# Decode attention on one core: value loads on a second queue, loads emitted four steps ahead, and the softmax maximum on TensorE

## The chip, the cores and the metric

The kernel runs on one core of a Trainium2 chip. The metric is device time in microseconds (us), as the median of several executions. The span on a profile page is one execution as the hardware profiler saw it; it is about 2 us shorter than the timed number. Most executions of a kernel agree within a per cent. An execution that is over 1.5% above the fastest of the same kernel is called slow and is left out of ratios.

## The reference, cut to what matters

One token attends over the last 4096 positions of a cache with 32 heads of size 128. A small MLP runs beside it, and its output gates the result.

```python
def _A_ref(x, k_cache, v_cache, wq, wo):          # x: 1 x 1 x 512
    W = min(4096, max(256, Sk // 4))              # Sk = 32768, W = 4096
    q = (x @ wq) ...                              # 32 heads x 128
    k = k_cache[:, :, Sk - W:, :]                 # 32 x 4096 x 128, bf16
    v = v_cache[:, :, Sk - W:, :]
    scores = einsum("bhqd,bhkd->bhqk", q, k) * Dh ** -0.5
    p = softmax(scores)
    return einsum("bhqk,bhkd->bhqd", p, v) ... @ wo
# ... the MLP is cut
return attention(layernorm(x)) * silu(mlp(x))
```

Keys and values are 32 x 2 tiles of 1 MiB. Each is read once and used for a few microseconds.

## The kernel before

Heads are taken in eight groups of four (`G = 4`). The scores of an even head are computed on VectorE. Those of an odd head take 32 transposes on TensorE, copies on ScalarE and 32 matrix-vector products. After the fourth key of a group comes the softmax. Values follow four heads later (`LAG = 4`). I write K28 for the key tile of head 28 and V28 for its value tile; "the Exp of group 6" is the softmax exponential of heads 24 to 27.

```python
def load(dst, src):
    return tc.keep_in_program_order(nc.sync.dma_start(out=dst, in_=src))   # all on SP's queue
...
def k_head(h, kn):
    if h % 2 == 0:                                   # VectorE: multiply, then sum over d
        nc.vector.tensor_tensor(out=prod[:], in0=kn[:], in1=q_bc[...], op=ALU.mult)
        nc.vector.tensor_reduce(out=s["sS"][...], in_=prod[:], axis=AX.X, op=ALU.add)
    else:                                            # TensorE transposes, ScalarE copies
        for b in range(NB):
            for i in range(8):
                nc.tensor.transpose(pt[:, i, :], kn[:, b * 8 + i, :], ident_bf[:])
            nc.scalar.copy(out=kt[:, b * 8:(b + 1) * 8, :], in_=pt[:])
        ...                                          # then qk(): 32 small matmuls
    if hl == G - 1:
        softmax(g)

def softmax(g):
    ...                                              # m1: maxima of each partition
    nc.gpsimd.partition_all_reduce(mb[:], m1[:], channels=P, reduce_op=ReduceOp.max)
    ...                                              # subtract, then on ScalarE:
    nc.scalar.activation(out=pT[:], in_=e[:], func=ACT.Exp, scale=scale)
...
for i in range(H + LAG):
    if i < H:
        k_head(i, load_kv(k_pool, A_k_cache, i))     # 12 key buffers
    ...
    if i >= LAG:
        h = i - LAG
        v = load_kv(v_pool, A_v_cache, h)            # 7 value buffers
        ...
        v_head(h, v)                                 # 32 matmuls of one head
```

So all loads stand in one queue, in the order in which they are needed: K4, V0, K5, V1 and so on.

## Time and profile before

| | before |
|---|---|
| time, median of 3 first runs | 198.48 us (198.36 to 199.85) |
| span of the profiled execution | 196.8 us |
| bytes moved | 79.17 MB |
| busy: TensorE, VectorE, ScalarE, GpSimd | 61%, 64%, 35%, 3% |
| mean granted TensorE clock | 0.667 of full speed |

The page of the kernel before shows how the loads are spread. A queue line gives packets, megabytes and the share of the 16 DMA engines' time. An issue line gives the count, the size of one and the median time from issue to landing:

```profile
q1 hardware_dynamic: 11176, 78.85, 96.3%
...
kv<-in_A_k_cache_dram SPq DMA_DIRECT2D x32, 1024.0 KB, 19.7
kv<-in_A_v_cache_dram SPq DMA_DIRECT2D x32, 1024.0 KB, 19.7
```

The reader should see one queue at 96% of the DMA engines' time, and a load that lands 19.7 us after its issue. At 424 GB/s a tile takes 2.47 us, so some eight loads are always in flight. The prediction shows three more views of this kernel: the strip (the span in 40 equal slices, with the busy share of the DMA engines in tenths and what they moved in GB/s), the ending chain (the work that ended last, followed back from step to step to what released it, as shares of the span), and the tail, which is the end of the timeline. The issue lines tell that keys and values are treated alike.

### The profile page before, as it was taken

Reading aid. Unit: us, or ns where it says so; the run is one execution under the profiler, and the core shown is the slowest. Engines: PE = TensorE matmul, PEld = TensorE weight load, DVE = VectorE, ACT = ScalarE, POOL = GpSimd, SP = SyncE. Lnnn points to the kernel's source line nnn. Section 1 sums busy time; section 2 is a strip of 40 time slices with the busy share of each in tenths; the row PEclk is TensorE's granted clock in tenths of the full one; section 3 lists DMA queues with packets and bytes.
Section 4 is the critical chain, followed back from the end, with each engine's and each line's share of the span. In section 5 each row is a group of like instructions: output and inputs, shape, how many; then the busy total and the mean of one; then the engine's idle time right before and its main releaser. Section 6 shows DMA issues by size and latency. Waiting matters only on the chain.

```text
span 196.8 us, 5237 instructions
## 1 busy us (share of the span) xinstructions
PE 119.4 (61%) x2399; PEld 108.4 (55%) x2399; DVE 126.9 (64%) x140; ACT 69.3 (35%) x82; POOL 4.9 (3%) x17
## 2 busy tenths in 40 slices
PE   0315896851969474684829293756665654929443
PEld 0314745841969473583829292656565653929332
DVE  1225049998959993959387937959198929594301
ACT  2000329742565243070707070242525250707000
POOL 1011000000000000000000000000000000000000
PEclk9999999695585555576766667555555585575555
DMA  6999899999999999999999999999999999999960
GB/s 185 383 485 446 355 416 421 426 426 421 426 421 423 421 421 425 423 425 420 426 421 428 421 425 416 425 420 426 423 428 423 425 418 425 421 426 422 426 268 10
DMA packets 11349, 79.17 MB, mean 402 GB/s; under 512 B 1376, under 2 KB 1984, under 8 KB 2368
## 3 DMA queue, kind: packets, MB, share of 16 engines
q1 hardware_dynamic: 11176, 78.85, 96.3%
q8 instruction: 18, 0.29, 0.6%
q10 hardware_dynamic: 152, 0.00, 0.0%
q14 instruction: 3, 0.02, 0.0%
HBM read 78.84 MB, written 0.00 MB: 401 GB/s over the span
## 4 chain that ended last, share of the span: by engine, by line
DMA 71%; DVE 12%; issue 6%; PE 6%; ACT 2%; POOL 1%; SPq 0%; POOLq 0%
DMA kv<-in_A_v_cache_dram 40%; DMA kv<-in_A_k_cache_dram 30%; DVE sS L265 7%; DVE prod L262 3%; ACT kt L272 1%; PE a_ps L202 1%; PE qT_ps L221 1%; PE oT L364 1%; PE qb_ps L230 1%; PE h_ps L135 1%; PE y_ps L135 0%; PE ln_ps L140 0%; PE ln_ps L152 0%; ACT q_bc L232 0%; POOL ln_rstd_x L158 0%
## 5 line engine op out<-in xcount | busy, mean ns | idle before, releaser
L272 ACT COPY kt<-pt 128x1024 bf16<-128x1024 bf16 x64 | 60.2, 1025 | 73.0 <-PE pt L271 73.0
L265 DVE TENSOR_REDUCE sS<-prod 128x32 f32<-128x4096 bf16 x16 | 70.7, 4419 | 0.5
L271 PE MATMUL pt<-ident_bf,kv 128*128 128x128 bf16 x512 | 53.8, 298 | 18.2 <-DMA kv<-in_A_k_cache_dram 17.7
L271 PEld LDWEIGHTS <-kv 128*128 128x128 bf16 x512 | 49.8, 140 | 19.7 <-DMA kv<-in_A_k_cache_dram 18.7
L364 PEld LDWEIGHTS <-kv 128*128 128x128 bf16 x1024 | 30.0, 102 | 30.5 <-DMA kv<-in_A_v_cache_dram 22.8
L262 DVE TENSOR_TENSOR prod<-kv,q_bc 128x4096 bf16<-128x4096 bf16 x16 | 36.5, 2283 | 11.0 <-DMA kv<-in_A_k_cache_dram 8.8
L364 PE MATMUL oT<-pT,kv 128*128 128x1 bf16 x1024 | 32.6, 165 | 17.6 <-DMA kv<-in_A_v_cache_dram 17.3
L243 PE MATMUL sT<-qT_bf,kt 128*128 128x1 bf16 x512 | 20.4, 166 | 2.6 <-ACT kt L272 2.3
L243 PEld LDWEIGHTS <-kt 128*128 128x128 bf16 x512 | 18.3, 103 | 3.4 <-ACT kt L272 3.2
L300 PE MATMUL den_ps<-pT,ones_bf 128*128 128x128 bf16 x8 | 2.0, 253 | 16.9 <-ACT pT L294 16.9
L371 DVE TENSOR_TENSOR o<-oT,rden 128x4 bf16<-128x4 f32 x7 | 1.1, 162 | 17.3 <-PE oT L364 17.3
L294 ACT ACTIVATE pT<-e 128x128 bf16<-128x128 f32 x8 | 2.5, 309 | 16.5 <-DVE e L290 16.5
L140 PEld LDWEIGHTS ln_ps<-x_f,ones_f 128*128 128x128 f32 x4 | 1.0, 312 | 11.3 <-DVE x_f L182 6.4
L287 POOL PARTITION_ALL_REDUCE mb<-m x8 | 3.0, 373 | 162.5 <-DVE m L285 162.5
L205 ACT ACTIVATE a_bf<-a_ps 128x10 bf16<-128x10 f32 x1 | 0.2, 180 | 17.4 <-PE a_ps L202 17.4
L302 DVE TENSOR_REDUCE den<-den_ps 128x4 f32<-128x128 f32 x8 | 2.3, 292 | 5.5 <-PE den_ps L300 5.5
L135 PEld LDWEIGHTS <-ox 128*1 128x1 bf16 x112 | 2.5, 113 | 5.3 <-DVE ox L341 5.3
L367 DVE TENSOR_TENSOR o<-oT,rden 128x1 bf16<-128x1 f32 x4 | 0.6, 161 | 7.2 <-PE oT L364 7.2
L230 PE MATMUL qb_ps<-wq_sb,xn_rep 128*128 128x512 bf16 x16 | 5.2, 497 | 0.0
L135 PE MATMUL y_ps<-wo,ox 128*1 128x128 bf16 x112 | 3.7, 306 | 2.3 <-DVE ox L341 2.3
L140 PE MATMUL ln_ps<-x_f,ones_f 128*128 128x4 f32 x4 | 1.2, 365 | 5.9 <-DVE x_f L163 4.9
L290 DVE TENSOR_TENSOR e<-sS,mb 128x64 f32<-128x64 f32 x8 | 1.8, 224 | 3.9 <-POOL mb L287 3.9
(79 smaller groups left out, 48.2 us busy)
## 6 DMA issues: line engine op xcount, KB each, us to landing
kv<-in_A_k_cache_dram SPq DMA_DIRECT2D x32, 1024.0 KB, 19.7
kv<-in_A_v_cache_dram SPq DMA_DIRECT2D x32, 1024.0 KB, 19.7
wq_sb<-in_A_wq_dram SPq DMA_DIRECT2D x1, 4096.0 KB, 19.2
wo<-in_A_wo_dram SPq DMA_DIRECT2D x3, 1024.0 KB, 20.4
w_sb<-in_B_w_dram SPq DMA_DIRECT2D x1, 1376.0 KB, 7.9
w_sb<-in_B_w_dram SPq DMA_DIRECT2D x1, 1024.0 KB, 10.2
w_sb<-in_B_w_dram SPq DMA_DIRECT2D x1, 512.0 KB, 3.7
wo<-in_A_wo_dram SPq DMA_DIRECT2D x1, 512.0 KB, 19.8
```

The costliest lines, as they stand in the source:

```text
L135: nc.tensor.matmul(ps[32 * j:32 * j + 1, :], lhsT=col, rhs=w[0:k, j * P:(j + 1) * P], start=False, stop=last, skip_group_check=True)
L140: nc.tensor.matmul(ps[:], lhsT=ones_f[:], rhs=src_f, start=True, stop=True)
L230: nc.tensor.matmul(qb_ps[:], lhsT=xn_rep[:, c, :], rhs=wq_h[:, c, 2 * i:2 * i + 8:2, :], start=(c == 0), stop=(c == KC - 1))
L243: nc.tensor.matmul(sT[:, hl // 2, c:c + 1], lhsT=kt[:, c, :], rhs=qT_bf[:, h:h + 1], start=True, stop=True)
L262: nc.vector.tensor_tensor(out=prod[:], in0=kn[:], in1=q_bc[:, h // 2:h // 2 + 1, :].to_broadcast([P, NC, Dh]), op=ALU.mult)
L265: nc.vector.tensor_reduce(out=s["sS"][:, hl // 2, :], in_=prod[:], axis=AX.X, op=ALU.add)
L271: nc.tensor.transpose(pt[:, i, :], kn[:, b * 8 + i, :], ident_bf[:])
L272: nc.scalar.copy(out=kt[:, b * 8:(b + 1) * 8, :], in_=pt[:])
L287: nc.gpsimd.partition_all_reduce(mb[:], m1[:], channels=P, reduce_op=ReduceOp.max)
L294: nc.scalar.activation(out=pT[:], in_=e[:], func=ACT.Exp, scale=scale)
L302: nc.vector.tensor_reduce(out=den[:], in_=den_ps[:], axis=AX.X, op=ALU.add)
L364: nc.tensor.matmul(oT[:, k:k + 1], lhsT=v[:, c, :], rhs=s["pT"][:, hl % 2, hl // 2, c:c + 1], start=(c == 0), stop=(c == NC - 1))
```

## The change

It has three parts. Keys stay on SP's queue and values go to ScalarE's (ACT), which should let two issuers work side by side. Loads are emitted four loop steps ahead of their use. The maximum over partitions goes from GpSimd's all-reduce to a transpose and a matmul on TensorE.

```diff
-    def load(dst, src):
-        return tc.keep_in_program_order(nc.sync.dma_start(out=dst, in_=src))
+    def load(dst, src, q=None):
+        return tc.keep_in_program_order((q or nc.sync).dma_start(out=dst, in_=src))
 ...
+    ident_f = const.tile([P, P], FP32, name="ident_f")
+    make_identity(nc, ident_f[:])
 ...
-        nc.gpsimd.partition_all_reduce(mb[:], m1[:], channels=P, reduce_op=ReduceOp.max)
+        mt_ps = ps_misc.tile([G, P], FP32, tag="misc", name="mt_ps")
+        nc.tensor.transpose(mt_ps[:], m1[:].rearrange("p a b -> p (a b)"), ident_f[:])
+        mx = sm_pool.tile([G, 1], FP32, tag="mx", name="mx")
+        nc.vector.tensor_reduce(out=mx[:], in_=mt_ps[:], axis=AX.X, op=ALU.max)
+        md = sm_pool.tile([G, G], FP32, tag="md", name="md")
+        nc.vector.tensor_scalar(out=md[:], in0=ident_f[0:G, 0:G], scalar1=mx[:], ...)
+        mb_ps = ps_misc.tile([P, G], FP32, tag="misc", name="mb_ps")
+        nc.tensor.matmul(mb_ps[:], lhsT=ones_f[0:G, :], rhs=md[:], start=True, stop=True)
+        nc.vector.tensor_copy(out=mb[:], in_=mb_ps[:].rearrange("p (a b) -> p a b", a=2))
 ...
+    def loads(i):
+        if i < H:
+            kt_in[i] = load_kv(k_pool, A_k_cache, i, nc.sync)
+        if LAG <= i < H + LAG:
+            h = i - LAG
+            vt_in[h] = load_kv(v_pool, A_v_cache, h, nc.scalar)
 ...
+    for i in range(PF):                              # PF = 4
+        loads(i)
 ...
     for i in range(H + LAG):
+        loads(i + PF)
 ...                                                  # k_head and v_head as before
```

More of the change, by code (lines that the diff above doesn't have):

```diff
@@ L7 @@
 from concourse.masks import make_identity
-from concourse.bass_isa import ReduceOp
 P = 128
@@ L21 @@
 LAG = 4
+PF = 4
 K_BUFS = 12
@@ L90, with load_kv @@
     load(wq_sb[:], A_wq.rearrange("(p c) n -> p c n", p=P))
-    def load_kv(pool, cache, h):
+    def load_kv(pool, cache, h, q):
         t = pool.tile([P, NC, Dh], BF16, tag="kv", name="kv")
-        load(t[:], cache[0, h, W0:, :].rearrange("(p c) d -> p c d", p=P))
+        load(t[:], cache[0, h, W0:, :].rearrange("(p c) d -> p c d", p=P), q)
         return t
@@ L286, in softmax @@
         mb = sm_pool.tile([P, 2, G // 2], FP32, tag="mb", name="mb")
-        nc.gpsimd.partition_all_reduce(mb[:], m1[:], channels=P, reduce_op=ReduceOp.max)
+        mt_ps = ps_misc.tile([G, P], FP32, tag="misc", name="mt_ps")
[3 more added lines that the diff above has]
+        md = sm_pool.tile([G, G], FP32, tag="md", name="md")
+        nc.vector.tensor_scalar(out=md[:], in0=ident_f[0:G, 0:G], scalar1=mx[:], scalar2=None,
+                                op0=ALU.mult)
+        mb_ps = ps_misc.tile([P, G], FP32, tag="misc", name="mb_ps")
+        nc.tensor.matmul(mb_ps[:], lhsT=ones_f[0:G, :], rhs=md[:], start=True, stop=True)
+        nc.vector.tensor_copy(out=mb[:], in_=mb_ps[:].rearrange("p (a b) -> p a b", a=2))
         e = sm_pool.tile([P, 2, G // 2, NC], FP32, tag="e", name="e")
@@ L382, in v_head @@
             later.append(step)
-    v_pool = None
-    for i in range(H + LAG):
+    kt_in, vt_in = {}, {}
+    def loads(i):
         if i < H:
-            k_head(i, load_kv(k_pool, A_k_cache, i))
-        if i == LAG:
-            wts_guard.__exit__(None, None, None)
-            v_pool = ctx.enter_context(tc.tile_pool(name="v", bufs=V_BUFS))
-        if i >= LAG:
+            kt_in[i] = load_kv(k_pool, A_k_cache, i, nc.sync)
+        if LAG <= i < H + LAG:
             h = i - LAG
-            v = load_kv(v_pool, A_v_cache, h)
+            vt_in[h] = load_kv(v_pool, A_v_cache, h, nc.scalar)
             if h + 1 in (b[0] for b in blocks):
@@ L398 @@
                 load_wo(last_block)
-            v_head(h, v)
+    for i in range(PF):
+        loads(i)
+    wts_guard.__exit__(None, None, None)
+    v_pool = ctx.enter_context(tc.tile_pool(name="v", bufs=V_BUFS))
+    for i in range(H + LAG):
+        loads(i + PF)
+        if i < H:
+            k_head(i, kt_in.pop(i))
+        if i >= LAG:
+            v_head(i - LAG, vt_in.pop(i - LAG))
     for t in range(blocks[last_block][1]):
```

## The prediction

> **What bounds the kernel now.** I read the strip of 40 slices first, then the chain that ended last, then the groups of instructions, and last the timeline of the tail. From the page of the kernel before:
>
> ```profile
> DMA  6999899999999999999999999999999999999960
> GB/s 185 383 485 446 355 416 421 426 426 421 426 421 423 421 421 425 423 425 420 426 421 428 421 425 416 425 420 426 423 428 423 425 418 425 421 426 422 426 268 10
> ...
> DMA 71%; DVE 12%; issue 6%; PE 6%; ACT 2%; POOL 1%; SPq 0%; POOLq 0%
> ```
>
> The DMA engines are full from about 2.5 us to about 190.4 us, at a steady 424 GB/s; the uneven slices two to five average about the same, so I read them as packets booked to a neighbouring slice, not as a gap. 71% of the ending chain is the landing of keys and values. 79.17 MB at 0.424 MB/us is 187 us; about 2.5 us of start and 5 us of tail (last value landed, its 32 matmuls, output) make the span of 196.8 us. The timed median of 198.48 us is 1.7 us over that span. So nothing on an engine can win more than fragments of the 10 us at the two ends, while anything that delays the last loads, or leaves work behind them, is paid in full.
>
> The groups give the unit costs that I use:
>
> ```profile
> L272 ACT COPY kt<-pt 128x1024 bf16<-128x1024 bf16 x64 | 60.2, 1025 | 73.0 <-PE pt L271 73.0
> L265 DVE TENSOR_REDUCE sS<-prod 128x32 f32<-128x4096 bf16 x16 | 70.7, 4419 | 0.5
> ...
> L262 DVE TENSOR_TENSOR prod<-kv,q_bc 128x4096 bf16<-128x4096 bf16 x16 | 36.5, 2283 | 11.0 <-DMA kv<-in_A_k_cache_dram 8.8
> ...
> L287 POOL PARTITION_ALL_REDUCE mb<-m x8 | 3.0, 373 | 162.5 <-DVE m L285 162.5
> ```
>
> Columns after the bars are busy us and mean ns, then idle before. An even key head costs VectorE 2.28 + 4.42 = 6.7 us; an odd one about 3.6 us of transposes and 3.8 us of ScalarE copies. Four loads (two key, two value heads) take 4 x 2.47 = 9.9 us, so all engines have room. The all-reduce to be removed is eight times 0.37 us; the timeline shows 0.79 us from the last maximum to the subtraction (182.53 to 183.32).
>
> The tail, from the timeline:
>
> ```profile
> 164.83 7.72 SPq L74 DMA_DIRECT2D kv<-in_A_v_cache_dram  x4
> ...
> 177.13 3.60 PE L271 MATMUL pt<-ident_bf,kv 128*128 128x128 bf16 x32 [1.49 <-DMA kv<-in_A_k_cache_dram]
> ...
> 183.71 0.31 ACT L294 ACTIVATE pT<-e 128x128 bf16<-128x128 f32 x1 [1.69 <-DVE e L290]
> ...
> 191.93 1.01 PE L364 MATMUL oT<-pT,kv 128*128 128x1 bf16 x32 [1.45 <-DMA kv<-in_A_v_cache_dram]
> ```
>
> SP has issued the last four values by 172.5 us, the last key is transposed at 177, the last softmax is out at 184, 8 us before the last value lands. After that landing only one head (1.0 us), 0.6 us of output rows and 3.3 us of finish remain.
>
> **What the Trainium skill says.** "DMA: Bandwidth & Descriptors", section "Issuing engines are not separate DMA queues": loads from several engines run on the same 16 DMA engines, and a second issuer saves only sequencer time. The trace agrees as far as one queue goes: SP alone holds 424 GB/s and an issue takes it 0.33 us per 2.47 us, so there is nothing to save. The same page, "Queues, rings and completion order": each DMA engine takes turns between the queues that have work. One queue of loads before cannot show that; I assume half the rate each while both have work. The same page, "Anatomy of one DMA — SWDGE (gpsimd) path": DMA engines do not wait on semaphores, the issuing sequencer does. The trace agrees for SP (59 us of waits on keys and 59 us on values). It means that a value load on ACT waits behind ScalarE's work, and ScalarE's work behind it.
>
> **The change part by part.**
>
> *Removed:* the all-reduce, 8 x 0.37 us on an idle engine. *Added:* per softmax an f32 transpose, a maximum, a scaling, an f32 matmul and a copy. From the f32 layer-norm matmuls (0.31 us weight load, 0.365 us matmul) and small VectorE operations of 0.15 to 0.2 us I estimate 0.65 + 0.2 + 0.2 + 0.6 + 0.2 = 1.9 us in place of about 0.5, so +1.4 us per group, and now in the in-order streams of TensorE and VectorE. Seven lie under DMA; one or two can lie in the tail.
>
> *Moved:* the order of the built kernels shows more than the diff. Eight completion counters are shared by both queues, as before by one, so about eight loads stay in flight. But keys can run 12 buffers ahead on SP, and ScalarE's stream places the value loads in fours behind exponentials: V4 to V7 come after the key copies of head 11 and the Exp of group 0; V24 to V27 after the Exp of group 5; V28 to V31 after the Exp of group 6. So keys lead, and the values are left over for the end. Early, this costs no bytes: I laid out issues and landings by hand with 2.47 us per load (twice that when both queues are busy). V0 goes out at about 31 us, as before, with 3 MB of keys still queued (three more key loads have passed it). V4 goes out only near 70 us, but SP then holds four or more key loads, so DMA stays full. The same holds until the keys end near 157 us.
>
> *The tail, where it counts.* (1) When the keys and output weights are done, V24 to V31 remain: 8.4 MB, 19.8 us. By bytes V23 therefore ends at 190.4 - 19.8 = 170.6 and is seen at about 172 us. It cannot be much earlier at 424 GB/s. (2) The Exp of group 6 needs the product of V23 first (VectorE's stream puts the output of group 5 ahead of that maximum), then the scores of K27, half the transposes of K29, and the new maximum through TensorE: 1.0 + 0.35 + 1.8 of transposes, 1.1 until the copies catch up, 1.6 of scores and transposes, 0.65 to the maximum, 2.5 for the new steps and subtraction, together about 9 us: Exp of group 6 at 181. (3) From there TensorE does, in this order, the denominators 0.3, V24 to V27 4.1, output weights of the third block 1.0, the rest of K31's transposes 2.7 with 1.9 until copied and scored, maximum and Exp of group 7 3.0: about 13 us, to 194. (4) Then denominators 0.3, V28 to V31 4.0, output rows and waits 1.9, finish 3.3: 9.5 us. Span 203.5. V28 to V31, issued from 181, move by about 192.5 and are seen by 194, so they no longer end it: compute does. (5) One term may add: the Exp of group 5, from the landing of K28 (about 149) through two VectorE heads and two softmaxes, comes out at 168 to 170, so V20 to V23 may be multiplied 1 to 2 us after V23 is there. I take +0.5.
>
> Sum: 196.8 + (203.5 - 196.8) + 0.5 = 204.0 span, +1.7 = 205.7 us: 3.6% slower.
>
> **The rivals.** *A, hidden anyway:* both kernels stay at the DMA bound and the tail is as before, 198 to 200 us. For it: 95% DMA occupancy, large engine slack. Against it: TensorE's stream puts K31's scores behind V27 and the last softmax is then about 10 us later. *B, faster:* two queues close gaps, the loads start sooner, 196 to 197.5 us. For it: SP did stall on the weight buffer until 30.1 us before V0. Against: the DMA strip has no hole there, and the last byte cannot move by over about 1 us. *C, worse:* ScalarE, held at a value load that waits for a key's landing (V14, V15 and V19 wait for K20, K21 and K27, as eight counters go round both queues), starves TensorE of copies and the whole DMA for some us; 209 to 214 us. For it: such a hold of nearly 10 us comes out of my layout twice. Against: SP had four loads queued each time. *D, two queues are slower or faster at the memory:* 1% of 187 us is 2 us either way; no trace here shows it.
>
> **Range and chances.** A smaller tail chain by 2 us and a rate 0.5% better give about 202.5; a late Exp of group 5 plus one starved stretch give 210. I take 202 to 210.5. Faster by over 2% (under 194.5) would need the tail gone: 2%. Within 2% (to 202.4) is rival A or half my tail: 17%. Slower: 81%.
>
> **What would show it.** Right: DMA strip full until about slice 35, with ScalarE's last value issues near 181 to 184 us; TensorE's key transposes of the last head after V27's matmuls; last Exp near 194; the ending chain with TensorE, VectorE and ACT in its last 20 us and DMA's share below 71%. Step 1 is wrong if V23 lands far from 172; step 2 if the Exp of group 6 is before 178; step 3 if it is not some 13 us before the last Exp. The whole is wrong if the last value landing still ends the chain, or if holes appear in the DMA strip before 150 us (rival C).

## The result

| | before | after |
|---|---|---|
| time, median of 5 | 198.65 us (198.36 to 199.85) | 204.32 us (203.79 to 207.33) |
| span of the profiled execution | 196.8 us | 203.6 us |
| mean granted TensorE clock there | 0.667 | 0.644 |

The ratio is 1.0286, with a 95% interval of 1.0228 to 1.0344: slower. Ratios here are the mean time of one kernel's fast runs over that of the other's fast runs of the same rounds, so they are not quite the ratios of the medians. One of the five runs of after (207.33) is slow and is left out of the ratio. The profiled execution was itself a longish one: it timed 205.76 us, and the other fast executions of after have spans of 201.6 to 202.1 us.

From the page of the kernel after, the strip, the queues, the ending chain, groups and issues:

```profile
DMA  6999999999999999999999999999999999979910
GB/s 218 401 450 409 410 422 417 425 417 420 420 422 415 422 418 420 422 423 418 417 423 420 417 417 425 420 423 417 417 423 418 413 411 341 420 328 362 417 52 3
...
q1 hardware_dynamic: 6568, 45.29, 53.9%
q10 hardware_dynamic: 4760, 33.56, 40.2%
...
DMA 61%; PE 21%; DVE 12%; issue 2%; SPq 1%; ACT 1%; ACTq 0%; DVEq 0%
...
L267 DVE TENSOR_REDUCE sS<-prod 128x32 f32<-128x4096 bf16 x16 | 70.6, 4412 | 0.2
...
kv<-in_A_k_cache_dram SPq DMA_DIRECT2D x32, 1024.0 KB, 19.2
kv<-in_A_v_cache_dram ACTq DMA_DIRECT2D x32, 1024.0 KB, 14.5
```

The work is the same: the longest VectorE group has the same mean, 4412 ns against 4419 ns. The bytes are the same too, now in two queues. What differs is the end. The strip falls to 341, 328 and 362 GB/s in slices 34, 36 and 37, and the last two slices hold almost no transfer. TensorE's share of the ending chain went from 6% to 21%. DMA's went from 71% to 61%. One more thing is easy to pass over: the middle of the strip is mostly around 420 where that of before is mostly around 424.

ScalarE's timeline in the tail of after shows when values were asked for. ACTq lines are its DMA issues; a bracket gives idle time and what ended it:

```profile
169.93 0.31 ACT L306 ACTIVATE pT<-e 128x128 bf16<-128x128 f32 x1
169.99 0.82 ACTq L74 DMA_DIRECT2D kv<-in_A_v_cache_dram  x2
...
182.33 0.31 ACT L306 ACTIVATE pT<-e 128x128 bf16<-128x128 f32 x1 [0.70 <-DVE e L302]
182.34 1.33 ACTq L74 DMA_DIRECT2D kv<-in_A_v_cache_dram  x2
...
183.74 0.92 ACTq L74 DMA_DIRECT2D kv<-in_A_v_cache_dram  x2
...
194.18 0.31 ACT L306 ACTIVATE pT<-e 128x128 bf16<-128x128 f32 x1 [3.02 <-DVE e L302]
```

V28 to V31 are asked for only after the Exp of group 6, at 182.34. Before had issued its last values by 172.5. The last Exp is at 194.18, against 183.71 before.

TensorE's timeline of after, from the last transposes on:

```profile
187.07 1.04 PE L376 MATMUL oT<-pT,kv 128*128 128x1 bf16 x32
...
188.18 1.87 PE L273 MATMUL pt<-ident_bf,kv 128*128 128x128 bf16 x16
...
191.91 0.37 PE L291 MATMUL mt_ps<-ident_f,m 128*4 128x128 f32 x1 [0.32 <-DVE m L287]
192.90 0.58 PE L298 MATMUL mb_ps<-md,ones_f 4*128 4x4 f32 x2 [0.62 <-DVE md L295]
...
194.60 1.03 PE L376 MATMUL oT<-pT,kv 128*128 128x1 bf16 x32
...
198.71 1.00 PE L376 MATMUL oT<-pT,kv 128*128 128x1 bf16 x32
```

V27's products (187.07) stand ahead of half the transposes of K31 (188.18). The maximum of the last group goes over TensorE at 191.91 and 192.90. V28's products start at 194.60, right after the last Exp, and V31's at 198.71. None of these lines has a DMA in its bracket: the tail is now computation. The critical view, which lists the ending chain in order of time, shows how far back that goes. Its last landing is that of K28:

```profile
128.12 21.68 DMA kv<-in_A_k_cache_dram
...
149.82 2.29 DVE prod L264
```

From 149.8 us to the end, 54 us, the chain holds only work of the engines and short gaps, although the DMA engines stay full until about 168 us.

### The profile page after: what moved, and what is told of

It is laid out like the page before. It is cut to its first block, busy times and chain, and to the rows that moved or that the text cites.

```text
span 203.6 us, 5299 instructions
## 1 busy us (share of the span) xinstructions
PE 119.7 (59%) x2423; PEld 108.5 (53%) x2423; DVE 128.2 (63%) x164; ACT 71.2 (35%) x82; POOL 2.3 (1%) x11
## 4 chain that ended last, share of the span: by engine, by line
DMA 61%; PE 21%; DVE 12%; issue 2%; SPq 1%; ACT 1%; ACTq 0%; DVEq 0%
DMA kv<-in_A_k_cache_dram 27%; DMA kv<-in_A_v_cache_dram 24%; DMA wq_sb<-in_A_wq_dram 10%; PE pt L273 7%; PE oT L376 5%; DVE sS L267 5%; DVE prod L264 4%; PE qb_ps L232 3%; PE sT L245 2%; PE y_ps L137 2%; SPq L74 1%; PE mb_ps L298 1%; ACT kt L274 1%; PE qT_ps L223 1%; PE mt_ps L291 1%
## 5 line engine op out<-in xcount | busy, mean ns | idle before, releaser
L267 DVE TENSOR_REDUCE sS<-prod 128x32 f32<-128x4096 bf16 x16 | 70.6, 4412 | 0.2
L273 PE MATMUL pt<-ident_bf,kv 128*128 128x128 bf16 x512 | 58.5, 287 | 14.9 <-DMA kv<-in_A_k_cache_dram 11.2
L273 PEld LDWEIGHTS <-kv 128*128 128x128 bf16 x512 | 46.2, 131 | 16.5 <-DMA kv<-in_A_k_cache_dram 11.8
L376 PEld LDWEIGHTS <-kv 128*128 128x128 bf16 x1024 | 29.8, 103 | 27.4 <-DMA kv<-in_A_v_cache_dram 13.8
L376 PE MATMUL oT<-pT,kv 128*128 128x1 bf16 x1024 | 30.7, 165 | 14.1 <-DMA kv<-in_A_v_cache_dram 13.2
L291 PE MATMUL mt_ps<-ident_f,m 128*4 128x128 f32 x8 | 3.1, 382 | 17.0 <-DVE m L287 17.0
L293 DVE TENSOR_REDUCE mx<-mt_ps 4x1 f32<-4x128 f32 x8 | 2.2, 277 | 7.3 <-PE mt_ps L291 7.3
L234 ACT CAST q_bc<-qb_ps 128x512 bf16<-128x512 f32 x4 | 2.3, 586 | 10.3 <-PE qb_ps L232 10.3
L298 PEld LDWEIGHTS mb_ps<-md,ones_f 4*128 4x128 f32 x16 | 3.8, 291 | 3.5 <-DVE md L295 2.7
L298 PE MATMUL mb_ps<-md,ones_f 4*128 4x4 f32 x16 | 4.5, 347 | 2.0 <-DVE md L295 2.0
L223 PE MATMUL qT_ps<-xn_bf,wq_sb 128*128 128x1 bf16 x64 | 1.9, 165 | 5.7 <-DMA wq_sb<-in_A_wq_dram 5.7
L223 PEld LDWEIGHTS <-wq_sb 128*128 128x128 bf16 x64 | 1.8, 104 | 6.0 <-DMA wq_sb<-in_A_wq_dram 6.0
```

Source lines behind the costliest of these rows:

```text
L223: nc.tensor.matmul(qT_ps[:, h:h + 1], lhsT=wq_sb[:, c, h * Dh:(h + 1) * Dh], rhs=xn_bf[:, c:c + 1], start=(c == 0), stop=(c == KC - 1))
L267: nc.vector.tensor_reduce(out=s["sS"][:, hl // 2, :], in_=prod[:], axis=AX.X, op=ALU.add)
L291: nc.tensor.transpose(mt_ps[:], m1[:].rearrange("p a b -> p (a b)"), ident_f[:])
L298: nc.tensor.matmul(mb_ps[:], lhsT=ones_f[0:G, :], rhs=md[:], start=True, stop=True)
L376: nc.tensor.matmul(oT[:, k:k + 1], lhsT=v[:, c, :], rhs=s["pT"][:, hl % 2, hl // 2, c:c + 1], start=(c == 0), stop=(c == NC - 1))
```

## The experiments

All times are medians of all runs of a kernel, with its slow runs if it had any. Each ratio is against the kernel before, run on the same chip. All runs passed the comparison with the reference. Single-part kernels come first, then those that test a cause.

### The maximum alone (e1)

The kernel before, with only the change of the maximum: `ident_f`, the transpose, the matmul and the three small VectorE operations.

```diff
-        nc.gpsimd.partition_all_reduce(mb[:], m1[:], channels=P, reduce_op=ReduceOp.max)
+        nc.tensor.transpose(mt_ps[:], ...)  # and so on, as in the change
```

> The kernel before with the maximum over TensorE and nothing else of the change. Tail theory (the values queue behind ScalarE's exponentials, so work is left after the last landing): the last softmax was out 8 us before the last value landed, so the slower maximum hides: 198.3 to 199.3 us, ratio to before 0.998 to 1.005, DMA at 424 GB/s in the middle. Rival 'maximum' (the two extra TensorE steps in in-order streams are the cost): 202 to 205 us. Rival 'rate' (two queues move 1% less): no change, 198.5.

Measured: 200.42 us, ratio 1.0083 (1.0053 to 1.0113). It is 1.7 us slower than before and above my range, with the last Exp at 186.23 and the last value landing still ending the chain. That could be the new steps, but the windows view says otherwise: the rate from 40 to 140 us is 420 GB/s instead of 424. The softmax sits under the transfers, so something slowed the transfers themselves. Experiment e9 below finds it.

### Everything but the maximum (e2)

```diff
 (after)
-        nc.tensor.transpose(mt_ps[:], ...)  # and so on
+        nc.gpsimd.partition_all_reduce(mb[:], m1[:], channels=P, reduce_op=ReduceOp.max)
```

> The changed kernel with the GpSimd all-reduce put back. Tail theory: only the softmaxes that stand one after the other in the tail (groups 6 and 7, perhaps 5) get 1.2 to 1.4 us shorter each: 200.5 to 203 us. Rival 'maximum': back to 198.5 to 199. Rival 'rate': stays near 203.5 to 204, less the 2 to 3 us of the two softmaxes only if they stand in the tail; DMA at 420 GB/s in the middle.

Measured: 206.66 us (204.76 to 207.78), ratio 1.0389 (1.0324 to 1.0455). The rival that the maximum is to blame falls: without it the kernel is no faster. My own figure is missed too. The place of the buffers (e9 below) is no excuse: in its built kernel e2 has its value buffers where before has them, and it moves 422 GB/s from 40 to 140 us. Its timeline of TensorE shows two stops inside runs of equal matmuls; "issue" means that the profile shows nothing that it waited for:

```profile
176.79 0.48 PE L272 MATMUL pt<-ident_bf,kv 128*128 128x128 bf16 x3 [1.72 <-issue]
...
190.00 0.72 PE L365 MATMUL oT<-pT,kv 128*128 128x1 bf16 x22 [2.08 <-issue]
```

Both stops lie in its compute tail, 3.8 us in sum, where after had one of 0.51 us. Its built order (the order in which the built program gives an engine its instructions) also puts 24 transposes of K31 behind V27, where after has 16. The two effects make e2 a poor measure of what the maximum costs in the tail. A packet of about 1 us in the instruction queue comes shortly before each of the two, but such packets come about every 10 us in e2 and in after, and most are followed by no stop. So late instructions are only my guess, and no run tests it.

### Values back on SP, the rest as after (e3)

```diff
 (after)
-            vt_in[h] = load_kv(v_pool, A_v_cache, h, nc.scalar)
+            vt_in[h] = load_kv(v_pool, A_v_cache, h, nc.sync)
```

> The changed kernel with the values back on the SP queue; emission 4 steps ahead and the TensorE maximum stay. Tail theory: K and V alternate in one queue again, nothing waits behind an exponential, the last key is copied before V27 is needed: 198 to 199.5 us and the last Exp some 8 us before the last landing. Rival 'emission ahead' (emitting 4 steps ahead is what hurts): 203 or more. Rival 'rate': 424 GB/s in the middle again and 198.5.

Measured: 200.27 us, ratio 1.0067 (1.0028 to 1.0106). One word in the code takes the kernel from 1.0286 to 1.0067, that is about 4.4 us (0.0219 of 198.7). The last Exp is at 186.27, as early as in e1:

```profile
186.27 0.31 ACT L306 ACTIVATE pT<-e 128x128 bf16<-128x128 f32 x1 [2.88 <-DVE e L302]
```

So the early emission does no harm by itself, and the second queue is what costs the larger part. What is left equals e1 within the error, at the same 420 GB/s; for that reason the time is above my range.

### Only the last eight values on SP (e7)

```diff
 (after)
-            vt_in[h] = load_kv(v_pool, A_v_cache, h, nc.scalar)
+            vt_in[h] = load_kv(v_pool, A_v_cache, h, nc.sync if h >= 24 else nc.scalar)
```

> The changed kernel with only the last eight value loads (heads 24 to 31) on SP, where no exponential stands ahead of them; in the built order K31's transposes now come ahead of V24's matmuls. Two queues work until about 160 us as in the changed kernel. Tail theory: most of the loss goes, 199.5 to 202 us, the last Exp well before 194 us after the span's start. Rival 'rate' (two queues are slower throughout, and that is the loss): 203 to 204.5. DMA at 420 GB/s in the middle in both.

Measured: 207.86 us, ratio 1.0455 (1.0417 to 1.0492). This is a miss, and the edit is to blame: it makes a new wait. SP's queue in the timeline of e7:

```profile
127.60 0.33 SPq L74 DMA_DIRECT2D kv<-in_A_k_cache_dram  x1
158.43 0.33 SPq L74 DMA_DIRECT2D kv<-in_A_v_cache_dram  x1
```

SP issues nothing for 31 us. V24 stands at the head of its queue and needs the buffer of V17, which is freed only after group 4's softmax. K29 and later keys wait behind it. The strip falls to 181 and 171 GB/s in slices 30 and 31. So e7 says nothing on the tail of after. It says that a load placed early in a queue, whose buffer comes free late, holds everything behind it.

### Values moved by 192 bytes (e9)

The new tiles of the change (`ident_f`, `mx`, `md`) come before the value buffers in memory. In the built kernels, value buffers start on a multiple of 512 bytes in before and 192 bytes past one in after, e1 and e3. Key buffers start 320 bytes past one in before and after alike. This kernel is before, with nothing new but an unused tile. All that lies behind the tile moves with it; of what is loaded from 40 to 140 us, that is the values.

```diff
 (before)
+    pad_v = ctx.enter_context(tc.tile_pool(name="pad_v", bufs=1)).tile([P, 96], BF16, name="pad_v")
+    nc.vector.memset(pad_v[:], 0.0)
```

> The kernel before with an unused block of 192 bytes per partition ahead of the value buffers, so that they start 192 bytes past a multiple of 512 bytes, as they do by accident in the changed kernel and in e1 (in the kernel before they start on a multiple; the key buffers start 320 past one in all). TensorE's order is that of before. Layout theory (the 1% lower rate of all kernels with the TensorE maximum comes from where their buffers start, not from the maximum): 420 GB/s between 40 and 140 us and 200.0 to 200.6 us, as e1. Rival 'work' (the extra TensorE and VectorE steps, or the missing GpSimd call, lower it): 424 GB/s and 198.4 to 198.9 us.

Measured: 200.28 us, ratio 1.0082 (1.0055 to 1.0108), the same as e1. The windows view from 40 to 140 us for before, where the last figure of a line is GB/s:

```profile
40.00:140.00 100.00, 63.90 (x1335) 60.74 (x1336) 75.68 (x62) 40.22 (x46) 1.87 (x5) 0.61 1.01 424
```

The same for e9:

```profile
40.00:140.00 100.00, 63.68 (x1304) 60.40 (x1305) 75.09 (x62) 39.39 (x46) 1.87 (x5) 0.57 1.01 419
```

TensorE, VectorE and ScalarE do the same work in both (63.90 and 63.68 us and so on). Only the rate differs. The 1.7 us of e1 are therefore the place of the value buffers, and the new maximum itself costs nothing where the kernel is bound by transfers.

### Keys and values on multiples of 512 bytes (e10, e12)

```diff
 (e10: before; e12: after; each with tiles that move both pools)
+    pad_k = ... .tile([P, 96], BF16, name="pad_k")
+    pad_v = ... .tile([P, 160], BF16, name="pad_v")     # e12: [P, 64]
```

> The kernel before with unused blocks of 192 and 320 bytes, so that key and value buffers all start on multiples of 512 bytes. Layout theory: the keys gain what the values lost in e1 or e9, 4 GB/s: 427 to 428 GB/s, 196.6 to 197.6 us, faster than both kernels. Rival 'work', or a layout effect of the values alone: 424 GB/s and 198.4 to 198.9 us.

Measured for e10: 197.81 us (22 runs) beside 198.46 us (27 runs), ratio 0.997 (0.9951 to 0.9989), rate 425 GB/s. It is 0.3% faster than before, which is less than I had expected (427 to 428 GB/s). No other version here is clearly faster than before.

> The changed kernel with its key and value buffers on multiples of 512 bytes; instruction order as in the changed kernel. Layout theory with the tail theory: rate 427 GB/s, V23 is there some 3 us earlier, but the tail from it is compute: 200.5 to 203 us, so still slower than before. Rival 'rate is all of the loss': 197 to 199 us. Rival 'layout does nothing': 204.

Measured for e12: 203.18 us (201.32 to 206.53, one of four slow), ratio 1.0191 (1.0138 to 1.0244). Its windows line reads:

```profile
40.00:140.00 100.00, 54.35 (x1058) 51.11 (x1059) 83.34 (x69) 31.93 (x36) 0.00 (x0) 0.53 1.01 425
```

So after with two queues also reaches 425 GB/s when its buffers start well. Two queues are not slower at the memory. By the medians of the fast runs (204.24 and 202.62) 1.6 us of after's loss goes away with the layout, and by the ratios 0.95%, or 1.9 us. The intervals are nearly as wide as that, so the size is rough. The remaining 1.9%, or 3.8 us, is not layout.

### Values through GpSimd's queue (e6)

If the loss comes from value loads that wait behind exponentials on ScalarE, an issuer that is idle otherwise should cure it.

```diff
 (after)
-            vt_in[h] = load_kv(v_pool, A_v_cache, h, nc.scalar)
+            vt_in[h] = load_kv(v_pool, A_v_cache, h, nc.gpsimd)
```

> The changed kernel with the values issued by GpSimd, which computes nothing here after the start, so no load waits behind an exponential; counters of its own. In the built order all keys are worked off ahead of V24 and the last Exp stands ahead of V28. Tail theory: 199.5 to 202 us (the 1% of rate stays), last Exp at least 5 us before the last landing. Rival 'two queues as such are the loss': 203.5 or more; so too if GpSimd's issuing is slow, which the issue-to-landing times would show.

Measured: 206.28 us, ratio 1.0375 (1.0339 to 1.0411). It does not cure it, and that is the most useful miss. The issues on the page of e6, then two lines of its TensorE timeline:

```profile
kv<-in_A_k_cache_dram SPq DMA_DIRECT2D x32, 1024.0 KB, 35.6
kv<-in_A_v_cache_dram POOLq DMA_DIRECT2D x32, 1024.0 KB, 19.0
```

```profile
169.11 0.61 PE L273 MATMUL pt<-ident_bf,kv 128*128 128x128 bf16 x4 [9.61 <-DMA kv<-in_A_k_cache_dram]
...
195.34 0.27 PE L312 MATMUL den_ps<-pT,ones_bf 128*128 128x128 bf16 x1 [1.06 <-ACT pT L306]
```

Now the values come early and the keys late: a key lands 35.6 us after its issue, and TensorE stands for 9.61 us before 169.11 until one is there. The last Exp is at 194.98, as late as in after, though no value ever waited behind ScalarE. In after the values were late, in e6 the keys. What the two have in common is two queues whose landings do not follow the fixed order in which the engines use them. In e3, with one queue in the order of use, the last Exp comes at 186.27.

### A quarter of the products of V24 to V27 (e16, e17)

This tests whether the tail of after is computation. The edit leaves out 96 of the 128 matmuls between the Exp of group 6 and that of group 7 (four heads use a quarter of the positions; the outputs still passed the tolerance). e16 is after with it, e17 is before with it. Their outputs are wrong, which doesn't matter for the times.

```diff
-        for c in range(NC):
+        cs = NC // 4 if 24 <= h < 28 else NC
+        for c in range(cs):
             nc.tensor.matmul(oT[:, k:k + 1], ...,
-                             start=(c == 0), stop=(c == NC - 1))
+                             start=(c == 0), stop=(c == cs - 1))
```

> The changed kernel with 96 of the 128 value matmuls of heads 24 to 27 left out (wrong result on purpose; their loads stay, and ScalarE's order is that of the changed kernel). They took 3 us between the Exp of group 6 and the Exp of group 7. Tail theory (TensorE's work left behind the last landing ends it): the Exp of group 7 moves from 194.2 to about 191 us and the whole by 2 to 3 us, to 201 to 202.5 us. Rival 'DMA still ends it': no change, 203.5 to 204.5.

> The kernel before with the same 96 matmuls left out (wrong result on purpose). There they lie under the DMA: no change, 198.2 to 198.9 us. If it gains 2 us too, the tail reading of the changed kernel's loss is wrong.

Measured: e16 202.47 us, ratio 1.0204 (1.0159 to 1.0249). That is 1.8 us under after by the medians of the fast runs (204.24 for after) and 1.6 us by the ratios, whose intervals overlap a little. e17 198.18 us, ratio 0.9989 (0.9971 to 1.0007), no change. ScalarE's timeline of e16 has the last Exp at

```profile
190.77 0.31 ACT L306 ACTIVATE pT<-e 128x128 bf16<-128x128 f32 x1 [2.70 <-DVE e L302]
```

instead of 194.18. The Exp of group 6 is at 181.57 there, so the stretch between the two Exps went from 11.85 us (194.18 − 182.33; in e12 it is 11.87) to 9.20. A head of 32 products takes TensorE 0.83 us in the chain of after, so the 96 left out are about 2.5 us, and 2.65 us came off. The same matmuls are free in before and paid for in after: that shows the tail of after to be computation.

The granted clock was not the same in the two traces, and this rival must be looked at. In that stretch it was 0.61 in after and 0.98 in e16, by the windows view, and 16 equal transposes took 1.87 us in after and 1.05 in e16. From these transposes to the last Exp, however, it is 6.00 us in after and 5.78 in e16, and e16 has waits of its own before them. Two single runs at the same mean clock (0.655) took 204.15 us (after) and 202.43 us (e16). So most of the gain is that of the matmuls, but the close fit of 2.5 and 2.65 is partly luck.

The transfers are not far behind the computation. In after, V31 was issued at about 184.3 and landed 11.8 us later, at about 196.1. That is 4 us later than the last landing of before (191.93), partly because it was asked for late (before had asked for its last by 172.5) and partly by the lower rate. It is only 2.6 us before TensorE takes it up at 198.71. In e16 TensorE waits 0.37 us for V31, and the ending chain is 76% DMA again. So I estimate from these times that less computation in the tail could give back at most about 2.6 us; the rest would need earlier requests.

### ACT queue without early emission (e4)

A larger dose of the same cause: before, with values on ScalarE's queue, emitted where they are used.

```diff
 (before)
-            v = load_kv(v_pool, A_v_cache, h)
+            v = load_kv(v_pool, A_v_cache, h, nc.scalar)
```

> The kernel before with the values on the ACT queue alone: no emission ahead, no TensorE maximum, layout as before. In the built order V23 to V26 stand behind the Exp of group 6 and V27 to V31, five loads, behind the last Exp. Tail theory: the last Exp cannot be before about 182 us, and from it two us of latency, five loads of 2.47 us and 5 us of finish remain: 203 to 209 us. Rival 'emission ahead is what hurts': 198.5 to 200.

Measured: 225.02 us, ratio 1.1316 (1.1253 to 1.1379). The direction is right and the size is far above what I expected. The page of e4 and ScalarE's timeline at its end:

```profile
DMA  6999999999999999999999999999908906935970
```

```profile
200.59 0.31 ACT L294 ACTIVATE pT<-e 128x128 bf16<-128x128 f32 x1 [2.55 <-DVE e L290]
200.59 2.50 ACTq L74 DMA_DIRECT2D kv<-in_A_v_cache_dram  x5
```

The strip has empty slices in its last quarter. SP has issued all keys by 137 us and the output weights by 143. In the last 56 us each group of values is issued only after an Exp (165.53, 184.02, 200.59), is moved, is multiplied, and only then comes the next Exp. Transfer and computation take turns. The early emission of after hides most of this: from e4 to after, which has the other maximum too, it is 21 us by the medians.

### Values through GpSimd, twelve heads behind (e18)

If the order of landing is the cause, keys further ahead of the values should take the softmax out of the tail also with two queues. (The softmax pool gets five buffers in place of three, as more groups are open.)

```diff
 (e6)
-LAG = 4
+LAG = 12
-    sm_pool = ctx.enter_context(tc.tile_pool(name="sm", bufs=3))
+    sm_pool = ctx.enter_context(tc.tile_pool(name="sm", bufs=5))
```

> Values on GpSimd as in e6, and the value work moved 12 steps behind the key work instead of 4 (5 small buffers instead of 3), so that the last key is worked off and the last Exp is out before V20 in TensorE's order. Narrow theory (only loads that stand behind exponentials are the loss): 199.5 to 201 us. Wider theory (two queues land keys and values in another order than the fixed order of the work, so work is left behind the last landing, whichever it is): twelve value heads of 1 us stand behind the last key in TensorE's stream: 202.5 to 206 us, with TensorE over 90% busy in the last 15 us and the last Exp well before 194 us.

Measured: 203.01 us, ratio 1.0214 (1.0182 to 1.0247). That is 3.3 us better than e6 by the medians, with the last Exp at 179.24, but its tail is not what I expected. TensorE's timeline of e18:

```profile
193.80 1.02 PE L376 MATMUL oT<-pT,kv 128*128 128x1 bf16 x32 [0.94 <-DMA kv<-in_A_v_cache_dram]
...
196.32 1.02 PE L376 MATMUL oT<-pT,kv 128*128 128x1 bf16 x32 [0.97 <-DMA kv<-in_A_v_cache_dram]
```

TensorE waits for landings again. The softmax is no longer in the tail, but the strip has a dip to 239 GB/s in slice 36. I read it as value buffers that come free late, because there are seven of them. GpSimd's timeline agrees: after 164.91 it issues no value until TensorE's products release it.

```profile
179.82 0.54 POOL L74 DMA_DIRECT2D kv<-in_A_v_cache_dram  x1 [14.37 <-PE oT L376]
```

No run with more buffers tests it. e18 agrees with the view that the order decides what ends the kernel. The time is in the range of my wider theory, but not for the reason I gave.

## Why the prediction was right, and where it was not

**The mechanism held.** It said 205.7 us, 202 to 210.5, slower. It came out at 204.32 us. The cause named, that values are left over for the end and computation after the last softmax takes the place of the last landing, is in the trace (last Exp at 194.18; chain with 21% TensorE; no DMA wait after it) and is shown by e3 and by the pair e16 and e17.

**The assumption on sharing** held. Each queue moves about 2.1 MB in 10 us while both have work, by the packets of the trace, half of the 4.2 MB that one queue moved before. This agrees with what the Trainium skill, "DMA: Bandwidth & Descriptors", section "Queues, rings and completion order", says of taking turns.

**Step 1** (V23 seen at about 172): it was issued at about 159 and landed 13.1 us later, at about 172; TensorE multiplied it at 173.4, without a wait for it. **Step 2** (Exp of group 6 at 181, or 181.5 with step 5): 182.33, with a stop of 0.51 us inside V23's products. **Step 3** (13 us to the last Exp, at 194): 11.9 us, at 194.18. **Step 4** (9.5 us to the end): 203.6 − 194.18 = 9.4 us. **Step 5** (Exp of group 5 at 168 to 170): 169.93. One time of step 4 was early: V31 was to be seen by 194 and landed at about 196.1. The addition for the new maximum, +1.4 us, also fits: from the last maximum of the partitions (191.62) to the subtraction (193.79) are 2.17 us, against 0.79 us before.

**The path was that of step 5, not of step 1.** The prediction let the landing of V23 set the Exp of group 6, and took +0.5 us for the case that V23 is there before TensorE is free. In after it is the other way round: the chain runs from the landing of K28 (149.80) over the Exp of group 5, and V23 lies ready for 1.3 us while TensorE is still at V20 to V22. In e12 the chain is the same. In e16 the two are so close that TensorE waits 0.35 us for V23. So step 1 gave a time that agreed, and not the wait that set the Exp. That the two come out together is luck.

**Two errors cancelled, and those are the terms to correct.** The sum held the rate at 424 GB/s; it was 420. Over the 187 us of transfers 1% is some 1.9 us. With the layout mended, e12 runs at 425 GB/s, has its V23 at about 169.5 instead of 172, its Exps of groups 6 and 7 at 179.40 and 191.27 and a span of 200.7. My layout of the tail was drawn for about that rate, so those are the numbers to hold it against: it is 2.7 us too long at the last Exp. Step 1 was 2.5 us too late. It took 170.6 from the bytes and allowed 1.4 us until V23 is seen. It also counted all output weights ahead of V23, but the last two of these loads (0.5 MB, 1.2 us at 424 GB/s) were issued by 150.7 in after and landed some 23.5 us later, behind V23; in e12 likewise. Step 2 was 0.9 us too short there (9.9 from V23's landing to the Exp, where I had 9); 1.3 of the 9.9 is V23 lying ready, which belongs to step 5, and the work itself took 8.6. Step 3 was 1.1 us too long (11.9, where I had 13). Also, the profiled execution was a long one (a span of 203.6, where the median of the fast ones is 202.05 and the prediction had 204.0), so its close fit with each time flatters the prediction.

**Rival D** ("two queues are slower or faster at the memory: 1%") had the size right and the cause wrong. 420 GB/s comes with one queue too (e1, e3, e9), and 425 with two (e12). The start of the buffers makes most of the difference. One rest stays unexplained: e2, with two queues and the buffers placed as in before, moved 422 where before moved 424. No part of the working looked at addresses.

**Rival A** (hidden anyway) fell by the interval of the result. **Rival B** (faster) fell too: the strip has no hole that a second queue could fill. **Rival C** (holds on ScalarE): they happen. The value issues at 84.25 take 10.85 us and those at 134.40 take 5.87 us, while ScalarE's copies wait. The strip has no hole there, as SP has keys in the queue. In e4, without keys in reserve, what rival C feared does come: empty slices.

**What the loss is made of.** After lies 5.7 us above before. By the ratios e3 puts 2.2% (4.4 us) on the second queue and leaves 0.7% (1.3 us). e12 puts 0.95% (1.9 us) on the layout and leaves 1.9% (3.8 us) to the rest. The two agree within their intervals. The maximum by itself is 0 where transfers bound the kernel (e1 equals e9).

**What stays open.** "Values wait behind exponentials" is one way to the loss, shown at a larger dose by e4, but e6 loses as much in another way. The wider statement, that two queues let the landings leave the order of use and so leave work behind the last softmax, covers after, e6 and e4. No run has two queues with landings held in the order of use, so it is argued and not shown. I drew it up after e6, and in e18 it had the time right but not what ended the kernel. How much of the 4 us is due to the 2.17 us maximum in the tail is not separated, because e2 changed the built order as well. The granted clock in the tail was not held fixed in any run. The stops of TensorE inside equal matmuls are not explained.

## What to carry to other kernels

When one queue already keeps the DMA engines full, a second one has nothing to add (here 420 GB/s with one or two queues, 425 with one or two once the buffers start well); what it changes is the order in which tiles land, so compare that order with the fixed order of the engines' work, and look first at the last two groups. A load issued by a computing engine waits behind that engine's waits, and a load whose buffer comes free late holds the queue behind it. When a change adds a small tile, compare the start addresses of the large buffers before you believe in any effect of 1%.

## What the Trainium skill lacked or had wrong

- "DMA: Bandwidth & Descriptors", section "Issuing engines are not separate DMA queues": it says that a second issuer only saves sequencer time. It does not say that it can cost: the same loads on SP alone gave 1.0067 (e3), shared with ScalarE 1.0286 (after), and without early emission 1.1316 (e4).
- The same page, section "How a descriptor splits into AXI transactions": it says that a transaction must start at a multiple of 256 bytes, so a descriptor that starts elsewhere costs more beats, and it speaks of reads, without saying whether the address of an SBUF destination counts in the same way. A rate that depends on where the SBUF destination starts is not there: value tiles 192 bytes past a multiple took 424 to 419 GB/s (e9), all tiles on multiples 425 (e10). As an estimate from that section, for a run of 8 KB in each partition: 262 beats instead of 256 with a start of 192, or 2.3% on half of the loads, about 1.2%; keys at 320, which is 64 past a multiple of 256, cost 258 beats, about 0.4%. The measured 1.2% (e9) and 0.3% (e10) are close. I made this estimate after the runs, so it is a candidate and not shown. e18 fits it: in its built kernel the values start 448 bytes past a multiple of 512, which is again 192 past one of 256, and e18 moved 420 GB/s from 40 to 140 us. No run has values at any other distance from a multiple of 256 than 0 or 192.
- Stops of TensorE inside runs of equal matmuls that wait for nothing in the profile, 0.51 us in after, 1.72 and 2.08 us in e2: I find no page that describes them. If my guess of late instructions is right, they belong to "Runtime: NRT & Kernel Launch", section "Instruction fetch mechanics", which gives no length for such a stop.
